# Attention and two MLP layers on one core: weight blocks without a cache in HBM, and a first down pass on half slabs

## The chip, the cores and the metric

One core of one Trainium2 chip runs the whole program. The metric is device microseconds of one execution, taken as the median of several runs; lower is better.

## The reference, cut to what matters

```python
# q, k, v: (4, 12, 448, 64); g_q, g_k: (64,); 1792 tokens of 768
q_n, k_n = rmsnorm(q, g_q), rmsnorm(k, g_k)
x = softmax(q_n @ k_n.T / 8) @ v          # per batch and head, then (1792, 768)
h = np.maximum(x @ w_in, 0.0)             # w_in  (768, 2048)
x = (h * h) @ w_out                       # w_out (2048, 768)
g = x @ w_gate                            # w_gate, w_val (768, 1536)
out = (g / (1 + np.exp(-g)) * (x @ w_val)) @ w_out2   # w_out2 (1536, 768)
```

The weights come in as 64-bit floats, so the kernel reads them as pairs of 32-bit words and builds 32-bit floats from them with integer operations. Each matrix product runs on TensorE in a reduced 32-bit format: an operand is split into a high part (rounded to that format) and a low part (the rest), and three products (high by high, high by low, low by high) are added up.

## The kernel before, in words

The kernel is one stream of instructions for each engine, in an order that is written out by hand in Python. Nothing is reordered later: an engine runs its own list in order and waits for other engines by semaphores. "Emitted" below means put at the end of such a list.

**Attention** (L363 to L796) runs over 24 pairs of heads, one iteration for each (the loop at L710). Per iteration TensorE makes a pass for the maxima (L543), the scores (L572), row sums (L608), transposes (L511, L552) and the product with v (L587, 16 matmuls). DVE (VectorE) reduces the maxima (L546, four per iteration) and makes the low parts of the transposed operands (L526, L530). POOL (GpSimd) normalises (L493) and adds up the exponentials (L578).

**The two up layers** (`up`, L940) use Strassen's scheme in Winograd's form: the weights of one quad (two slabs of 128 output columns, each 768 deep) are combined to seven blocks P1 to P7 of 128 x 384, and the tokens of a pair of batches (tp 0 or 1) to seven types B11, B21, B22, T1 to T4. A group is one block by one type: 9 matmuls of 128x128 by 448 columns (L871). The first layer has 8 quads, the second 12, so they have 112 and 168 groups. The types T1 to T4 need differences on DVE (`combine`, L120), a high part on ACT (ScalarE; L123) and a low part on DVE or POOL (L127), 1344 columns each. After a group DVE or ACT evicts PSUM (L834, L837). In before, the first two quads run for tp 0 alone at the start of a layer, and for tp 1 alone at its end. Their 14 blocks are made once, stored to HBM (`keep`, L281) and loaded twice through a ring of five buffers (`ring_loads`, L252 to L260).

**The two down layers** (`down`, L992) take the hidden blocks (128 x 448) back from HBM (`stage`, L967, L974), split each in `cleave` (L976: high part on ACT at L980, low part on POOL by the helper at L834) and multiply it with a split slab of weights: 18 matmuls (L1014) for one block, for four batches t after each other, over 16 or 12 slabs f. The slab of block (t=0, f) is converted just ahead of its use.

**Weights.** `stream` (L328) is a generator of all weight work: `convert` (L187) makes 32-bit floats of a slab of 128x768 by one ACT copy (L204) and three DVE operations (L206, L210, L214); sums of half slabs are made on DVE (L286); `block` (L270) splits a block by an ACT cast (L275) and a DVE subtraction (L276); `down_slab` (L315) splits a whole slab (L323 on ACT, L324 on DVE). `pump(budget)` (L343) emits the next operations of that generator up to a budget in planned microseconds; it is called after each group and each down step. In attention `prep_early(1)` (L351) does so for one DVE operation, at two places of each iteration from the third on:

```python
for c in range(NCH):
    if i > 0:
        maxpass(i + 1, c)
    scores(i, c)
    ...
    if c == 1:
        ...
        if i >= 3:
            prep_early(1)          # L732, in the middle of the scores
...
if i >= 3:
    prep_early(1)                  # L756, ahead of the row sums
```

Raw slabs are loaded by `load_raws` (L170, DMA issued at L180) into one buffer and a second that borrows space from the token array. All DMAs of the program but four tiny ones are issued in order by SP (SyncE); a wait ahead of one holds up those behind it.

Of the kernel before, what the change touches and what calls it, by code (L numbers as in the profile page):

```python
# [8 lines left out]
F32 = mybir.dt.float32  # L9
# [10 lines left out]
def kernel(  # L20
# [17 lines left out]
    P = 128  # L38
# [10 lines left out]
    RING = 5  # L49
    UNIT = 2 * KT * S  # L50
# [11 lines left out]

    def slot(s):
        return xacc[:, s * S:(s + 1) * S]
# [5 lines left out]
    units, flat = {}, {}  # L70

    def open_units(name, ids, side="left", apart=False):
        pool = ctx.enter_context(tc.tile_pool(name=name, bufs=1, side=side))
        for part in ([i] for i in ids) if apart else (ids,):
            t = pool.tile([P, len(part) * UNIT], F32R, tag=f"u{part[0]}", name=f"u{part[0]}")
            for n, i in enumerate(part):
                units[i] = t[:, n * UNIT:(n + 1) * UNIT]
            flat[part[0]] = t

    where = (  # L80
# [4 lines left out]
    )  # L85
    HUNIT = (10, 7)
    WHOME = ([(3, n) for n in range(7)] + [(0, n) for n in range(5)] + [(7, n) for n in range(4)],
             [(3, n) for n in range(7)] + [(11, 0), (12, 0), (13, 0), (0, 0), (0, 1)])
# [5 lines left out]
    free = []  # L94
    state = {"turn": 1, "used": 0, "raw": 0, "debt": 0.0, "late": False}
# [4 lines left out]

    def part_hi(t, kk):
        name = {(0, 0): "B11", (0, 1): "B21", (1, 1): "B22"}[t % 2, kk // KT]
        k = kind(0, t // 2, name)
        nc.scalar.copy(k[:, 0, kk % KT * S:(kk % KT + 1) * S], slot(t * KD + kk))

    def part_lo(t, kk, eng=None):
        name = {(0, 0): "B11", (0, 1): "B21", (1, 1): "B22"}[t % 2, kk // KT]
        k = kind(0, t // 2, name)
        cut = slice(kk % KT * S, (kk % KT + 1) * S)
        (eng or nc.vector).tensor_tensor(  # L110
            out=k[:, 1, cut], in0=slot(t * KD + kk), in1=k[:, 0, cut].bitcast(F32), op=ALU.subtract
        )

    def combine(tp, name, eng=None):
# [5 lines left out]
        (eng or nc.vector).tensor_tensor(out=slots3(*o), in0=slots3(*a), in1=slots3(*b), op=ALU.subtract)  # L120

    def hi3(name, tp, ph=0):
        nc.scalar.copy(kind(ph, tp, name)[:, 0], home3(tp, name))  # L123

    def lo3(name, tp, ph=0, eng=None):
# [4 lines left out]
        if name[0] == "T":  # L130
            t, h = home[name]
            s = (2 * tp + t) * KD + h * KT
            free.extend(x for x in range(s, s + KT) if not 12 <= x < 16 and x < 20)
            state["late"] |= (t, h, tp) == (1, 1, 1)

    def both(name, tp, ph=0, eng=None):
        hi3(name, tp, ph)
        lo3(name, tp, ph, eng)
# [13 lines left out]
    def row_slab(w, f):  # L152
        w, e = words(w)
        return w[f * P:(f + 1) * P, :].rearrange("p (a f) -> p a f", a=KD)
# [5 lines left out]
    raws, convs, ssum, ring = [], [], [], []  # L160
    slabs = []
    for ph in range(2):
        for n, (w, g) in enumerate(ups[ph]):
            for f in range(2):
                slabs.append((col_slab(w, 2 * g + f), 0 if n < 4 or f else 1))
        for f in range(NF[ph]):
            slabs.append((row_slab(downs[ph], f), 1 - f % 2))
# [921 lines left out]
```

## Time and profile before

| what | value |
|---|---|
| median of 3 runs | 1334.46 us (1333.95 to 1338.06) |
| the profiled execution's own time | 1340.05 us |
| its span in the profile | 1338.3 us |
| busy share of the span, PE / DVE / ACT / POOL | 91% / 55% / 42% / 37% |
| mean granted TensorE clock | 0.963 of full speed |
| moved by DMA | 166.81 MB |

Matmuls are pipelined, so the busy share of PE overstates its work; how many matmuls ran in a stretch says more. The shares of the other engines are averages over stages that have different limits: attention ends at about 290 us, the first up layer at 537, the first down layer at 817, the second up layer at 1156.

### The profile page before, as it was taken

To read this page: it belongs to the slowest core of one execution; us is meant where nothing else is said; L and a number is where in the kernel's file an instruction comes from. 1 tells how busy PE (TensorE), PEld (TensorE's weight loads), DVE (VectorE), ACT (ScalarE), POOL (GpSimd) and SP (SyncE) were. 2 spreads that over 40 slices of the span, in tenths; PEclk is the share of its full clock that TensorE was granted. 3 is DMA by queue.
4 is the path that set the end of the run, shared out by engine and by line. 5 is a ranking of instruction groups with operands and counts; after the bars stand their busy time and mean duration, and the time that the engine had idled before them with its cause. 6 is when DMAs were issued, how large, how long until landed. Compare 5 with 4: busy or idle time off the path is not lost.

```text
span 1338.3 us, 17283 instructions
## 1 busy us (share of the span) xinstructions
PE 1220.1 (91%) x6416; PEld 1018.4 (76%) x6416; DVE 731.9 (55%) x900; ACT 559.2 (42%) x917; POOL 500.8 (37%) x423
## 2 busy tenths in 40 slices
PE   8989888897799997976799999799999998799998
PEld 5555544466699996865599999699999997689998
DVE  7777878857767637766101104776776655740000
ACT  6767766563455544423122224333343332331221
POOL 6887877644010001221235456311302312333332
PEclk9999989898999998987799999899999999999999
DMA  5334444224334448746522213322233227643331
GB/s 161 109 114 130 125 119 134 87 90 142 126 103 142 158 128 281 227 155 216 184 77 62 62 42 95 108 97 80 89 102 110 89 73 240 226 139 102 110 106 46
DMA packets 109189, 166.81 MB, mean 125 GB/s; under 512 B 13105, under 2 KB 94769, under 8 KB 109105
## 3 DMA queue, kind: packets, MB, share of 16 engines
q1 hardware_dynamic: 108784, 165.71, 39.4%
q8 instruction: 50, 0.82, 0.3%
q14 instruction: 35, 0.28, 0.1%
q10 hardware_dynamic: 320, 0.00, 0.0%
HBM read 123.21 MB, written 42.29 MB: 124 GB/s over the span
## 4 chain that ended last, share of the span: by engine, by line
PE 42%; DVE 4%; DMA 3%; issue 2%; ACT 1%; POOL 0%; SPq 0%; POOLq 0%; ACTq 0%; DVEq 0%
PE ps L1014 22%; PE ps L871 20%; DMA keep<-ring 1%; DVE conv L210 1%; DMA xacc<-hid 1%; DVE xacc L120 1%; DVE conv L214 1%; DVE conv L206 1%; DMA xacc<-in_moe_w_out_dram 1%; ACT u L123 0%; DMA ring<-keep 0%; DMA raw<-in_moe_w_val_dram 0%; POOL u L834 0%; DVE xacc L834 0%; ACT conv L204 0%
## 5 line engine op out<-in xcount | busy, mean ns | idle before, releaser
L871 PE MATMUL ps<-u,ring 128*128 128x448 f32 x2520 | 538.8, 375 | 46.5 <-DVE xacc L834 27.4
L871 PEld LDWEIGHTS ps<-u,ring 128*128 128x128 f32 x2520 | 483.8, 193 | 101.7 <-DVE xacc L834 25.2
L1014 PE MATMUL ps<-u,u 128*128 128x448 f32 x2016 | 427.3, 373 | 32.2 <-ACT u L980 14.5
L1014 PEld LDWEIGHTS ps<-u,u 128*128 128x128 f32 x2016 | 386.4, 192 | 72.8 <-ACT u L980 18.7
L834 POOL TENSOR_TENSOR u<-xacc,u 128x448 fp32r<-128x448 f32 x112 | 134.3, 1202 | 322.3 <-ACT u L980 322.3
L834 POOL TENSOR_TENSOR xacc<-xacc 128x448 f32<-128x448 f32 x76 | 99.9, 1318 | 391.4 <-ACT xacc L837 274.5
L980 ACT CAST u<-xacc 128x448 fp32r<-128x448 f32 x112 | 63.2, 565 | 250.2 <-PE ps L1014 200.2
L1026 DVE COPY xacc<-ps 128x448 f32<-128x448 f32 x24 | 14.8, 623 | 270.6 <-PE ps L1014 270.6
L834 DVE TENSOR_TENSOR xacc<-ps,xacc 128x448 f32<-128x448 f32 x188 | 115.7, 619 | 79.4 <-PE ps L871 63.8
L578 POOL TENSOR_TENSOR sg<-p 112x896 f32<-112x896 f32 x46 | 97.9, 2130 | 40.4 <-ACT p L574 40.4
L546 DVE TENSOR_REDUCE mxz<-s 112x2 f32<-112x896 f32 x96 | 100.0, 1082 | 20.8 <-PE s L543 20.7
L276 DVE TENSOR_TENSOR ring<-conv,ring 128x384 fp32r<-128x384 f32 x100 | 69.8, 700 | 66.7 <-ACT ring L275 66.5
L837 ACT ACTIVATE xacc<-xacc 128x448 f32<-128x448 f32 x132 | 76.1, 576 | 66.5 <-DVE xacc L834 64.8
L837 ACT ACTIVATE xacc<-ps 128x448 f32<-128x448 f32 x108 | 58.0, 543 | 94.2 <-PE ps L871 70.2
L574 ACT ACTIVATE p<-s 112x896 f32<-112x896 f32 x96 | 87.5, 920 | 19.2 <-PE s L572 15.3
L275 ACT CAST ring<-conv 128x384 fp32r<-128x384 f32 x100 | 50.7, 509 | 77.7 <-PE ps L871 45.5
L587 PE MATMUL s<-p,v 112*64 112x448 f32 x384 | 80.0, 559 | 0.0
L572 PE MATMUL s<-th 64*112 64x448 f32 x576 | 76.5, 369 | 1.4 <-DVE th L530 0.8
L206 DVE TENSOR_SCALAR conv<-conv 128x768 int32<-128x768 int32 x68 | 51.8, 761 | 35.1 <-ACT conv L204 33.5
L127 POOL TENSOR_TENSOR u<-xacc,u 128x1344 fp32r<-128x1344 f32 x15 | 48.7, 3249 | 31.5 <-ACT u L123 27.5
L493 POOL TENSOR_TENSOR qk<-raw,r 112x512 f32<-112x512 f32 x46 | 59.9, 1306 | 1.0
L210 DVE SCALAR_TENSOR_TENSOR conv<-raw,conv 128x768 int32<-128x768 int32 x42 | 59.1, 1406 | 1.2
(75 smaller groups left out, 973.8 us busy)
## 6 DMA issues: line engine op xcount, KB each, us to landing
hid<-xacc SPq DMA_DIRECT2D x112, 224.0 KB
xacc<-hid SPq DMA_DIRECT2D x112, 224.0 KB
ring<-keep SPq DMA_DIRECT2D x56, 384.0 KB
keep<-ring SPq DMA_DIRECT2D x28, 384.0 KB
xacc<-in_moe_w_out_dram SPq DMA_DIRECT2D x14, 768.0 KB
raw<-in_moe_w_out_dram SPq DMA_DIRECT2D x14, 768.0 KB
raw<-in_moe_w_in_dram SPq DMA_DIRECT2D x12, 768.0 KB
raw<-in_moe_w_gate_dram SPq DMA_DIRECT2D x8, 768.0 KB
```

The costliest lines, as they stand in the source:

```text
L206: nc.vector.tensor_scalar(out=ci, in0=ci, scalar1=3, scalar2=0x7FFFFFFF, op0=ALU.logical_shift_left, op1=ALU.bitwise_and)
L210: nc.vector.scalar_tensor_tensor(out=ci, in0=high, scalar=-0x80000000, in1=ci, op0=ALU.bitwise_and, op1=ALU.bitwise_or)
L276: nc.vector.tensor_tensor(out=r[:, 1], in0=src, in1=r[:, 0].bitcast(F32), op=ALU.subtract)
L546: nc.vector.tensor_reduce(out=mxz[:, c, 0:P:D], in_=ps[:CP, :, :S], op=ALU.max, axis=AX.X)
L572: nc.tensor.matmul(ps[:CP, a, :S], lhs, rhs, start=(w == 0), stop=(w == 3))
L574: nc.scalar.activation(out=p, in_=ps[:CP, :, :S], func=AF.Exp)
L578: nc.gpsimd.tensor_tensor(out=sg, in0=p_t[pi, 2 * w], in1=p_t[pi, 2 * w + 1], op=ALU.add)
L587: nc.tensor.matmul(ps[s, :S], v_t[pi][:, a, c * D:(c + 1) * D], p[:, a, :], start=(c == 0), stop=(c == NCH - 1),)
L834: eng.tensor_tensor(out=o, in0=a, in1=b, op=op)
L837: nc.scalar.activation(out=slot(s), in_=src, func=func)
L871: nc.tensor.matmul(ps, w[:, wi, kk * P:(kk + 1) * P], xk[:, xi, kk * S:(kk + 1) * S], start=bool(first and mm == 0), stop=(mm == 3 * KT - ...
L1014: nc.tensor.matmul(ps[o], w[:, wi, o * P:(o + 1) * P], h[:, hi], start=(f == 0 and n == 0), stop=(f == nf - 1 and n == 2),)
```

## The change

The cache in HBM is gone. At the start of an up layer P1 and P2 of the first two quads run for tp 0 and then for tp 1, and all other blocks run for both pairs at once, straight from the ring. The types of tp 1 are therefore made in the first 18 groups, by a list of due groups. There are five conversion buffers instead of three. The raw buffer of attention is a tile of its own; later raws lie in the token array (slots 16 to 23).

In the down layers the weights come as half slabs (128 x 384). The first pass takes batches 0 and 1 together: for half 0 and then half 1 of the outputs, and for each f, both hidden blocks meet one half slab (2 x 3 outputs x 3 = 18 matmuls). Their hidden blocks are loaded and split twice, once for each half. Batches 2 and 3 follow with whole rows as before. The low part of a hidden block is made on DVE, no longer on POOL. In attention the first of the two `prep_early(1)` calls is left out, and T1 and T2 of tp 0 are split after it.

```diff
     for ph in range(2):
         for n, (w, g) in enumerate(ups[ph]):
...
-        for f in range(NF[ph]):
-            slabs.append((row_slab(downs[ph], f), 1 - f % 2))
+        for h in range(2):
+            for f in range(NF[ph]):
+                loads.append((row_half(downs[ph], f, h), ((h * NF[ph] + f) % 4,)))
...
+    def load_raws(lag=2):
+        while nsent["n"] < len(loads):
+            i = nsent["n"]
+            src, at_ = loads[i]
+            if i >= state["limit"] or i - len(turned) > 3 or not all(valid(b) for b in at_):
                 return
+            for n in range(max(0, i - 8), i):
+                if set(loads[n][1]) & set(at_) and turned.get(n, 1 << 30) + lag > clock["n"]:
+                    return
...
+            sent[i] = clock["n"]
...
+    def convert(i, c, cost):
...
+        arrived = lambda: i in sent and clock["n"] >= sent[i] + 3
...
+        yield act(lambda: nc.scalar.activation(out=c, in_=high.bitcast(F32), func=AF.Copy, scale=TINY), gate=arrived)
+        yield dve(0.6 * cost, lambda: nc.vector.tensor_scalar(
+            out=ci, in0=ci, scalar1=3, scalar2=0x7FFFFFFF, op0=ALU.logical_shift_left, op1=ALU.bitwise_and))
+        yield dve(cost, stt, ci, high, -0x80000000, ALU.bitwise_and)
+        yield dve(cost, stt, ci, low, 29, ALU.logical_shift_right)
+        turned[i] = clock["n"]
...
     def block(entry, src):
-        n = at[entry][0]
...
-        if how == "store":
-            c = cache[ph, p, q_] = mem["keep"].tile([P, 2 * KH], F32, tag=f"c{ph}{p}{q_}", name="keep")
-            nc.sync.dma_start(out=c, in_=r.bitcast(F32).rearrange("p h n -> p (h n)"))
-            used(n)
+        yield act(nc.scalar.copy, r[:, 0], src, gate=lambda: state["used"] >= n - RING + 1)
+        yield dve(0.55, minus, r[:, 1], src, r[:, 0].bitcast(F32))
...
+            for n in range(2 * NF[ph]):
+                c = convs[i % NCONV][:, :KH]
...
+                ops = convert(i, c, 0.5)
+                i += 1
+                op = next(ops)
+                yield op[:4] + (lambda g=op[4], n=n, ph=ph: g() and state["down"] >= 100 * ph + n // 6,)
+                for k, op in enumerate(ops):
+                    yield op
+                    if k == 1 and late:
+                        yield late
+                        late = None
...
+                yield act(nc.scalar.copy, t[:, 0], c)
+                late = dve(0.55, low_half, ph, n, t, c)
...
     def pump(budget):
         state["debt"] = min(state["debt"] + budget, budget + 1.5)
-        while state["debt"] > 0:
-            cost = next(steps, None)
...
+        while True:
+            op = peek()
+            if op is None or (op[4] and not op[4]()) or (op[0] == "dve" and state["debt"] <= 0):
                 return
-            state["debt"] -= cost
+            state["debt"] -= run_op()
...
             for i in range(np_):
+                clock["n"] += 5
+                load_raws()
...
-                        if i >= 3:
-                            prep_early(1)
...
-                elif i == np_ - 2:
-                    both("T1", 0)
-                elif i == np_ - 1:
-                    both("T2", 0)
...
         def up(ph):
...
-            for n, (p, q_) in enumerate(paired):
-                step(ph, [(p, q_, 0)], n0[0] + n)
...
+            todo = [("P1", 0, 0), ("P1", 1, 0), ("P2", 0, 0), ("P2", 1, 0),
+                    ("P1", 0, 1), ("P1", 1, 1), ("P2", 0, 1), ("P2", 1, 1)]
+            todo += [(p, q_, tp) for p, q_ in paired[4:] + mid for tp in range(2)]
+            last = len(ups[ph]) - 1
+            for p, q_, tp in todo:
+                step(ph, p, q_, tp, 1.0 if state["down"] < 100 * ph else 1.6)
...
         def cleave(ph, t, f):
...
             nc.scalar.copy(k[:, 0], src)
-            tt(nc.gpsimd, k[:, 1], src, k[:, 0].bitcast(F32), ALU.subtract)
+            tt(nc.vector, k[:, 1], src, k[:, 0].bitcast(F32), ALU.subtract)
...
         def down_open(ph):
...
+            dn_seq[:] = [[(t, f) for t in range(2)] for _ in range(2) for f in range(nf)]
+            dn_seq.extend([(t, f)] for t in (2, 3) for f in range(nf))
...
-                pump(3.2)
+                pump(2.1)
...
+        plan_types(0, [
+            (1, "h", 0, "T1", None), (1, "l", 0, "T1", None), (1, "h", 1, "B11", None), (1, "l", 1, "B11", None),
+            (2, "h", 1, "B21", None), (3, "h", 0, "T3", None), (3, "l", 0, "T3", g), (3, "l", 1, "B21", None),
+            (4, "c", 1, "T1", None), (5, "h", 1, "T1", None),
...
```

In the list at the end, "c" is a combination, "h" a high part on ACT, "l" a low part (on POOL where `g` stands, else on DVE), and the first number is the group after which it is emitted.

## Rows read from the trace of the kernel before

**Rows 1.** Stretches: engine busy and (records), PEclk, DMA share, GB/s
```profile
290.10:536.70 246.60, 221.59 (x1012) 197.81 (x1009) 159.80 (x215) 127.01 (x220) 40.18 (x27) 0.94 0.49 154
536.70:817.20 280.50, 250.50 (x1153) 224.03 (x1151) 86.15 (x93) 75.81 (x123) 96.96 (x69) 0.94 0.38 121
600.00:663.00 63.00, 40.85 (x150) 33.52 (x149) 27.29 (x36) 16.26 (x31) 10.35 (x9) 0.80 0.63 214
663.00:817.00 154.00, 153.65 (x753) 142.32 (x754) 12.74 (x12) 35.12 (x55) 70.97 (x49) 0.99 0.21 57
817.20:1157.00 339.80, 318.29 (x1521) 287.50 (x1520) 229.70 (x309) 124.30 (x210) 94.27 (x65) 0.98 0.37 120
850.00:1117.00 267.00, 267.00 (x1286) 242.44 (x1285) 175.06 (x255) 92.89 (x169) 65.02 (x52) 0.99 0.31 99
```

**Rows 2.** Timeline of PE in attention: the product with v of some iterations
```profile
32.47 3.23 PE L587 MATMUL s<-p,v 112*64 112x448 f32 x16
42.16 3.23 PE L587 MATMUL s<-p,v 112*64 112x448 f32 x16
...
99.35 3.23 PE L587 MATMUL s<-p,v 112*64 112x448 f32 x16
113.31 3.23 PE L587 MATMUL s<-p,v 112*64 112x448 f32 x16
122.95 3.23 PE L587 MATMUL s<-p,v 112*64 112x448 f32 x16
...
268.79 3.23 PE L587 MATMUL s<-p,v 112*64 112x448 f32 x16
```

**Rows 3.** Timeline of DVE in attention: weight steps
```profile
106.25 2.16 DVE L276 TENSOR_TENSOR ring<-ssum,ring 128x384 fp32r<-128x384 f32 x1 [1.14 <-ACT ring L275]
...
118.97 0.55 DVE L286 TENSOR_TENSOR conv<-conv,ssum 128x384 f32<-128x384 f32 x1
...
145.20 3.62 DVE L206 TENSOR_SCALAR conv<-conv 128x768 int32<-128x768 int32 x1
```

**Rows 4.** Timeline of PE: waits at the edges of the up layers
```profile
363.25 37.06 PE L871 MATMUL ps<-u,ring 128*128 128x448 f32 x166 [5.21 <-DVE xacc L834]
...
849.50 20.68 PE L871 MATMUL ps<-u,ring 128*128 128x448 f32 x90 [7.36 <-DVE xacc L834]
```

**Rows 5.** The chain that ended last, in the first down layer
```profile
636.20 4.04 DMA keep<-ring
```

**Rows 6.** Timeline of ACT and DVE in the first down layer: one weight slab
```profile
555.87 0.83 ACT L323 CAST u<-conv 128x768 fp32r<-128x768 f32 x1 [3.07 <-DVE conv L214]
...
556.61 0.91 ACT L204 ACTIVATE conv<-xacc 128x768 f32<-128x768 f32 x1
...
557.62 0.55 DVE L206 TENSOR_SCALAR conv<-conv 128x768 int32<-128x768 int32 x1
...
558.21 1.82 DVE L210 SCALAR_TENSOR_TENSOR conv<-xacc,conv 128x768 int32<-128x768 int32 x1
...
560.06 0.96 DVE L214 SCALAR_TENSOR_TENSOR conv<-xacc,conv 128x768 int32<-128x768 int32 x1
561.05 0.83 ACT L323 CAST u<-conv 128x768 fp32r<-128x768 f32 x1 [3.07 <-DVE conv L214]
```

**Rows 7.** Groups of instructions: busy us, mean ns, then idle before
```profile
L834 DVE TENSOR_TENSOR xacc<-ps,xacc 128x448 f32<-128x448 f32 x188 | 115.7, 619 | 79.4 <-PE ps L871 63.8 <-ACT xacc L837 8.1 <-POOL xacc L834 7.5
...
L980 ACT CAST u<-xacc 128x448 fp32r<-128x448 f32 x112 | 63.2, 565 | 250.2 <-PE ps L1014 200.2 <-DMA xacc<-hid 36.0 <-issue 13.3
...
L275 ACT CAST ring<-conv 128x384 fp32r<-128x384 f32 x100 | 50.7, 509 | 77.7 <-PE ps L871 45.5 <-DVE conv L214 19.9 <-DVE conv L286 6.9
L127 POOL TENSOR_TENSOR u<-xacc,u 128x1344 fp32r<-128x1344 f32 x15 | 48.7, 3249 | 31.5 <-ACT u L123 27.5 <-issue 3.5
...
L120 DVE TENSOR_TENSOR xacc<-xacc 128x1344 f32<-128x1344 f32 x16 | 37.4, 2339 | 33.2 <-POOL u L127 33.2
...
L286 DVE TENSOR_TENSOR conv<-conv,conv 128x384 f32<-128x384 f32 x20 | 11.0, 551 | 0.0
```

More of the change, by code (lines that the diff above doesn't have):

```diff
@@ L49 @@
     RING = 5
+    NCONV = 5
     UNIT = 2 * KT * S
@@ L93 @@
     home = {"B11": (0, 0), "B21": (0, 1), "B22": (1, 1), "T1": (0, 0), "T2": (1, 1), "T3": (1, 0), "T4": (0, 1)}
-    free = []
-    state = {"turn": 1, "used": 0, "raw": 0, "debt": 0.0, "late": False}
+    loose = set()
     def home3(tp, name):
@@ L130, in lo3 @@
         if name[0] == "T":
[L131 to L138, printed above, removed]
+            release(tp, name)
     def split(n):
@@ L168 @@
-    turned = {"slab": 0}
-    def load_raws():
-        while state["raw"] < len(slabs):
-            i = state["raw"]
-            src, r = slabs[i]
-            if (r == 1 and not state["late"]) or i > turned["slab"] + 1:
-                return
-            if any(slabs[n][1] == r for n in range(turned["slab"], i)):
-                return
-            dst = raws[r]
-            if src.dtype == I32:
-                nc.sync.dma_start(out=dst.rearrange("p (a f) -> p a f", a=KD), in_=src)
-            else:
-                nc.sync.dma_start(
-                    out=dst.bitcast(F32)[:, :KD * P].rearrange("p (a f) -> p a f", a=KD), in_=src
-                )
-            state["raw"] += 1
@@ L813, in moe @@
         due = []
-        clock = {"n": 0}
+        types = []
         def later(n, fn, *args):
@@ L911, in after @@
                 later(1, finish_sum, ph, q_, tp, ij, s)
-        def step(ph, group_args, n, extra=()):
-            for p, q_, tp in group_args:
-                group(ph, p, q_, tp, n)
-                if (p, q_, tp) == group_args[-1]:
-                    used(n)
-                clock["n"] += 1
-                run_due()
-                after(ph, p, q_, tp)
-                while drain and drain[0][0] <= clock["n"]:
-                    drain.pop(0)[1]()
-                if types:
-                    types.pop(0)()
-                pump(1.6 if ready["down"] >= 2 * ph else 1.0)
@@ L940, in up, with step @@
[L940 to L959 removed]
+        def step(ph, p, q_, tp, rate):
+            group(ph, p, q_, tp)
+            if tp == 1:
+                assert at[ph, p, q_] == state["used"]
+                state["used"] += 1
+            clock["n"] += 1
+            run_due()
+            load_raws()
+            while types and types[0][0] <= clock["n"]:
+                types.pop(0)[1]()
+            after(ph, p, q_, tp)
+            while drain and drain[0][0] <= clock["n"]:
+                drain.pop(0)[1]()
+            pump(rate)
@@ new lines, in up, with stage @@
+            for args in dn_seq[1]:
+                cleave(ph, *args)
+        dn, hl, dn_seq, dn_list = {}, {}, [], []
+        count = {}
+        held = {}
+        def stage(ph, upto):
+            nf = NF[ph]
+            while count["s"] < len(dn_list) and dn_list[count["s"]][0] <= upto:
+                i, t, f = dn_list[count["s"]]
+                if i < 2 * nf:
+                    s = next((s for s in free if 3 <= s < 6 or 9 <= s < 16), None)
+                    if s is None:
+                        return
+                    free.remove(s)
+                    held[t, f] = s
+                else:
+                    if i == 2 * nf:
+                        assert not any(set(a) & {2, 3} for n, (_, a) in enumerate(loads) if n in sent and n not in turned)
+                        loose.difference_update(range(20, 24))
+                    s = 20 + i % 4
+                dn[t, f] = slot(s)
+                nc.sync.dma_start(out=slot(s), in_=hid[ph][f, t])
+                count["s"] += 1
```

561 lines of the change are left out of this document (290 added, 271 removed), and 4 rows, old and new, of the table where.

## The prediction

> **What bounds the kernel now.** I began with the stretches, because the shares over the whole span mix stages with different limits. The reader should look for stretches in which the count of matmuls is as high as it gets: 1286 in 267.00 us in the middle of the second up layer, 0.2076 us each, and 753 in 154.00 us late in the first down layer, 0.2045 us each [rows 1]. There TensorE has no gap. At these rates the work of the MLP stages is 1008 x 0.2076 = 209.3 (first up), 1152 x 0.2045 = 235.6 (first down), 1512 x 0.2076 = 313.9 (second up) and 864 x 0.2045 = 176.7 us (second down). The first three stages last 246.6, 280.5 and 339.8 us [rows 1], so they lose 37.3, 44.9 and 25.9: 108.1 us in all. The second down layer loses nothing but its end. Neither DVE nor DMA is busy throughout: the loss lies at the edges of the stages.
>
> The timeline of PE then shows the edges: up layers wait 5 to 7 us at a time for DVE while the types are made [rows 4]. The chain of waits shows stores to the cache one after the other, this one of 4.04 us and four like it [rows 5], in a stretch of 63 us that ran 150 matmuls and had a granted clock of 0.80 [rows 1].
>
> Last I read attention by iterations. One without any weight step lasts 42.16 - 32.47 = 9.69 us, one with short steps 122.95 - 113.31 = 9.64, another 113.31 - 99.35 = 13.96 [rows 2]. What differs is the weight step in the middle of the scores: 0.55 us in the one, 2.16 us for the same 384 columns in the other [rows 3]; it stands ahead of two of the four maxima that TensorE needs next. The 19 iterations from 42.16 to 268.79 take 226.6 us [rows 2] where 19 x 9.7 is 184.3: 42 us lost.
>
> **The change, part by part.**
>
> *Attention: -34 us.* The step in the middle goes. Nine of the 19 iterations look like the one at 99.35, with a middle step of 1.25 to 4.79 us; together they are 35.5 us over 9.7. I take nearly that, 34. The other step stays: 12 conversion and 6 split operations, one per iteration, which fit (each of four slabs takes four iterations, load included). It is not free: one such step took 3.62 us [rows 3], four of 18 were over 3 us, and the low parts of the operands wait behind it; that iteration was 2.5 us too long. Bounds: 42 if everything goes, 15 if other operations are hit as often half the time. Moving T1 and T2 out costs nothing here and is counted below.
>
> *Start of the first up layer: 9 us lost in place of some 25.* No ring loads, and P1 and P2 need only types made early. New is a rush on ACT and DVE: within 18 groups three combinations at 2.34 us, five low parts on DVE, and six on POOL at 3.25 us [rows 7]. Three places can stop TensorE. The eviction of P2 of quad 1 takes a slot that POOL's first low part has just read; behind it on ACT stand T1's high part and the copies that the second P1 pair needs: some 2 us. T2 of tp 1 is emitted at group 10 behind T3 on DVE and needed at group 13: some 3. The raw slabs of quad 2 need slots that POOL's last low part reads; 6 x 3.25 and four additions put that at about 41 us, landing and conversion at 52 to 57, where group 28 starts at 28 x 1.87 = 52: some 4. That load waits on SP, and the stores of hidden blocks queue behind it; their slots are reused only some ten evictions later. Bounds: 2 and 20.
>
> *End of the first up layer and first pass of the first down layer: 16 us.* The stores and reloads go, and with them their waits. What comes is the half slab. In before a whole slab is a loop between ACT and DVE: cast, copy, three DVE operations, next cast, 561.05 - 555.87 = 5.18 us [rows 6], while 18 matmuls take 18 x 0.2045 = 3.68. The half has no row. From below its operations are half of the whole's, from above the same. DVE operations on 384 columns took 0.551 and the ACT cast 0.509 [rows 7], so I take 0.58 with the gap for three DVE operations, 0.53 for cast and copy, and 0.37 for the shift (whole: 0.55 [rows 6]). A half then is 0.37 + 3 x 0.58 = 2.11 us on DVE, and after its last operation DVE waits for cast and next copy, 1.06. The new pump gives 2.1 of planned 1.85 per half, that is 8 halves in 7 steps. Each step also has two hidden blocks: two ACT casts of 0.565 and, now on DVE, two subtractions of about 0.62 [rows 7]. Per step DVE is busy 8/7 x 2.11 + 2 x 0.64 = 3.69 and idle some 0.7, since the subtractions fill part of the 1.06. So a step lasts 4.4 us, 0.7 more than TensorE's.
>
> The halves begin ten groups before the end. With four raw buffers, each back after five to six groups, 7 are done by then; they and ten evictions take 7 x 2.7 + 6.2 = 25 us on DVE where TensorE has 10 x 1.87 = 18.7: 6.5 late. 25 halves are left, 22 steps, 22 x 0.7 = 15.4. The blocks are split two steps ahead, a lead of 2 x 3.68 - 1.85 = 5.5. Together 15.4 + 6.5 - 5.5 = 16. The change of half at step 16 needs six banks evicted with two free: 2 us more. Traffic is no bound: a step loads 2 x 224 + 8/7 x 384 = 887 KB in 4.4 us, 202 GB/s, where 214 were moved before [rows 1].
>
> [...]
>
> *Later passes of the first down layer: nothing.* One subtraction of 0.62 per step of 3.68 on DVE beside the next layer's weights; should its cover go, nine low parts on POOL could each hold it up to 3.25 us [rows 7].
>
> *First to second up layer: 4 us lost in place of some 12* [rows 4]. The same rush without the raws: T1 comes first, T2 is again close at group 13. Bounds 1 and 10.
>
> *End of the second up layer and its down layer: 12 us, and 2 for the change of half.* As above with 24 halves: 17 left, 15 steps, 10.5 + 6.5 - 5.5. Before it was some 16.
>
> Sum: losses after 9 + 16 + 2 + 4 + 12 + 2 = 45, against 108.1: -63. With attention -97. From the span of 1338.3 that is 1241.3; outside the span lay 1340.05 - 1338.3 = 1.75, so 1243 for such an execution. The median of the runs shown is 5.6 us below the profiled time, so I predict 1237.
>
> **The rivals.**
>
> (a) *The loop is hidden.* If the order on ACT and DVE leaves no idle time, a step takes 3.69 and the passes lose some 4 us each: 1237 - 20 = 1217. For it: DVE's busy time alone just fits. Against it: the whole-slab loop left DVE idle at each cast. Chance 0.14.
>
> (b) *Attention stays slow,* because the remaining step or the reductions themselves run into POOL as often: 1237 + 34 = 1271. For it: the step of 3.62 us [rows 3]. Against it: it stands beside the product with v, 3.23 us of TensorE [rows 2]. Chance 0.12.
>
> (c) *Subtractions held by POOL.* With the lead used up, nine low parts at 3.25 us [rows 7] cost 29 us: 1266. Against it: the lead recovers once the halves are done. Chance 0.06. [...]
>
> (d) *Slower than before.* The half costs what the whole did: 5.18 us of loop [rows 6], since fixed costs or late raws, not columns, set it. A step is then 8/7 x 5.18 + 1.85 = 7.8 us, and 37 steps lose 3.4 more each: 1237 + 125 = 1362. It decides from a step of 4.4 + 97 / 37 = 7.0 us on. Against it: 384 columns at 0.55 [rows 7]. Chance 0.05.
>
> (e) *The schedule isn't kept:* the four slabs aren't done when attention ends, since each waits for its load. Then the first groups wait for some 18 operations, 20 us: 1257. Chance 0.03.
>
> **How the numbers follow.** The forecast has 0.60 and 1237, with its own range 1212 to 1262 from the bounds of attention and the starts. The range over the cases: below, attention 42 and losses of 20, 1204; above, attention 15 and losses of about 80, 1290. Only (d) and the tails lie outside. A measurement of this kernel can tell about 0.3%, 4 us. All cases but (d) are faster: 0.92 with a little off for mixtures; 0.02 within, 0.06 slower.
>
> **What would show it.** Right: iterations of attention near 9.7 us all through, attention ending near 256 us; steps of about 4.4 us in both first passes with PE waiting for DVE's subtraction, ACT casts waiting for the third DVE operation; no wait of over 4 us at the starts of up layers; up-layer rate still 0.2076. Wrong: iterations of 12 us and more in attention; PE waiting for raw DMA or, late in a down layer, for subtractions that last over 2 us; steps of 3.7 us (then (a)) or over 5.

## The result and the profile after

| | before | changed |
|---|---|---|
| median | 1336.26 us (1333.95 to 1341.86, 4 runs) | 1260.87 us (1259.04 to 1263.33, 4 runs) |
| span of the profiled execution | 1338.3 us | 1259.1 us |
| its own time | 1340.05 us | 1261.24 us |
| busy PE / DVE / ACT / POOL | 91 / 55 / 42 / 37% | 95 / 64 / 47 / 30% |
| moved by DMA | 166.81 MB | 146.64 MB |

The ratio is 0.9431, interval 0.9396 to 0.9467. A first look at where the 79.2 us of span went is by the stretches of [rows 1], here from the kernel after: first up layer, first down layer, 19.5 steps of its first pass, second up layer, second down layer.

```profile
253.21:489.69 236.48, 212.96 (x1013) 193.58 (x1009) 164.02 (x240) 128.37 (x232) 51.68 (x29) 0.95 0.40 127
489.69:743.24 253.55, 243.31 (x1153) 217.12 (x1153) 131.26 (x229) 96.23 (x179) 28.50 (x9) 0.99 0.42 130
512.87:596.80 83.93, 76.98 (x352) 64.65 (x351) 60.77 (x122) 39.64 (x84) 0.00 (x0) 1.00 0.62 196
743.24:1061.55 318.31, 309.59 (x1514) 285.51 (x1512) 229.71 (x330) 122.75 (x220) 87.28 (x61) 0.98 0.31 99
1061.55:1259.10 197.55, 185.07 (x864) 163.92 (x864) 81.94 (x151) 58.28 (x115) 2.39 (x2) 0.98 0.43 137
```

Against [rows 1] attention is 36.9 us shorter (290.10 to 253.21), the first up layer 10.1, the first down layer 27.0, the second up layer 21.5; the second down layer is 16.3 longer, since its first pass now pays for the second layer's edge. Taking off the work at the prediction's rates (209.3, 235.6, 313.9 and 176.7 us), the four stages lose 27.2, 17.9, 4.4 and 20.9: 70.4, of which 4.6 were there before at the very end. So 65.8 stand against the 45 forecast. This is a net figure: where nothing held TensorE, its matmuls ran faster after the change than at the prediction's rates (last section), which hides about 11 us, an estimate from the starts of the groups; the edges themselves cost some 77.

The product with v in attention, the instruction of [rows 2]:

```profile
42.00 3.23 PE L609 MATMUL s<-p,v 112*64 112x448 f32 x16
51.70 3.23 PE L609 MATMUL s<-p,v 112*64 112x448 f32 x16
...
217.57 3.23 PE L609 MATMUL s<-p,v 112*64 112x448 f32 x16
229.86 3.23 PE L609 MATMUL s<-p,v 112*64 112x448 f32 x16
```

Nineteen iterations from 42.00 take 187.9 us where they took 226.6. Most are 9.7 long; the one ahead of 229.86 is the longest with 12.29. What stands in it on DVE is not the weight step but a combination (L124) beside POOL:

```profile
215.94 6.75 DVE L124 TENSOR_TENSOR xacc<-xacc 128x1344 f32<-128x1344 f32 x1
```

The waits of PE at the edges, where [rows 4] had 5.21 and 7.36 (the number in brackets is the idle time before the instruction, then what ended it):

```profile
259.04 3.93 PE L881 MATMUL ps<-xab,ring 128*128 128x448 f32 x18 [1.92 <-ACT xacc L849]
269.62 5.48 PE L881 MATMUL ps<-xbb,ring 128*128 128x448 f32 x18 [3.00 <-ACT xacc L849]
289.00 0.74 PE L881 MATMUL ps<-xbt,ring 128*128 128x448 f32 x1 [4.60 <-ACT xbt L141]
293.47 3.36 PE L881 MATMUL ps<-xbt,ring 128*128 128x448 f32 x8 [3.73 <-DVE xbt L145]
481.32 3.70 PE L881 MATMUL ps<-xat,ring 128*128 128x448 f32 x9 [8.06 <-DVE xacc L846]
489.69 0.47 PE L1058 MATMUL ps<-xat,xab 128*128 128x448 f32 x1 [2.00 <-ACT xat L1010]
497.13 3.27 PE L1058 MATMUL ps<-xat,xab 128*128 128x448 f32 x7 [3.01 <-ACT xat L1010]
565.80 0.88 PE L1058 MATMUL ps<-xat,xbb 128*128 128x448 f32 x3 [2.06 <-ACT xacc L1080]
...
1054.11 6.38 PE L881 MATMUL ps<-xat,ring 128*128 128x448 f32 x18 [7.32 <-ACT xat L367]
```

Four waits stand at the start of the first up layer. The longest, 8.06 and 7.32, stand ahead of the last groups of each up layer: an eviction (L846) and a half slab's cast (L367) that came late.

Some waits cost more than their own length. TensorE's granted clock stood at two levels from 253.21 us on, 1.00 in 3819 and 0.50 in 191 of 4024 windows of 0.25 us, and between them only in the 14 in which it changed; behind the wait of 8.06 us it stood at the lower one (the column after POOL's is the granted clock):

```profile
481.32:485.22 3.90, 3.70 (x10) 2.78 (x10) 2.39 (x5) 1.91 (x5) 0.00 (x0) 0.50 0.95 358
```

The nine matmuls that start at 481.32 last 3.70 us where nine take 1.82 to 1.86 at the full clock. The stretches from 293.47 to 296.60 (behind the waits of 4.60 and 3.73), from 497.13 to 501.00 (behind 3.01) and from 1054.10 to 1057.50 (behind 7.32) show 0.50 as well; in between, TensorE ran on and the rows are back at 1.00. An estimate from windows of 1 us, TensorE's busy time times what was missing of the full clock, gives some 16 us for the four stages after the change and some 29 before it.

What holds the start is on POOL, DVE and ACT:

```profile
261.91 4.45 POOL L145 TENSOR_TENSOR xat<-xacc,xat 128x1344 fp32r<-128x1344 f32 x1 [0.65 <-ACT xat L141]
263.87 3.90 DVE L124 TENSOR_TENSOR xacc<-xacc 128x1344 f32<-128x1344 f32 x1
266.40 0.55 ACT L849 ACTIVATE xacc<-ps 128x448 f32<-128x448 f32 x1 [4.11 <-POOL xat L145]
...
280.94 4.16 POOL L145 TENSOR_TENSOR xbb<-xacc,xbb 128x1344 fp32r<-128x1344 f32 x1 [4.92 <-ACT xbb L141]
285.13 2.47 DVE L124 TENSOR_TENSOR xacc<-xacc 128x1344 f32<-128x1344 f32 x1 [2.97 <-POOL xbb L145]
289.82 1.19 DVE L227 TENSOR_TENSOR ring<-conv,ring 128x384 fp32r<-128x384 f32 x1 [2.22 <-ACT ring L367]
290.93 2.48 DVE L145 TENSOR_TENSOR xbt<-xacc,xbt 128x1344 fp32r<-128x1344 f32 x1
```

The low part of T3 on POOL and the combination of T1 on DVE run beside each other and both last longer (3.25 and 2.34 on average in [rows 7]; a combination alone took 1.55 us in this trace); the eviction on ACT waits 4.11 us for POOL's slot, as forecast. The last four lines are the chain behind the waits of 4.60 and 3.73: the combination of T2 waits 2.97 us for POOL's low part of B22, and T2's own low part stands behind a weight operation (L227) that waits 2.22 us for ACT.

The loop of one half slab, which answers to the 5.18 us of [rows 6]:

```profile
528.53 0.51 ACT L367 CAST xbb<-conv 128x384 fp32r<-128x384 f32 x1 [2.11 <-DVE conv L224]
528.95 0.54 ACT L243 ACTIVATE conv<-xacc 128x384 f32<-128x384 f32 x1
529.39 1.02 ACT L1010 CAST xat<-xacc 128x448 fp32r<-128x448 f32 x2
529.52 0.36 DVE L244 TENSOR_SCALAR conv<-conv 128x384 int32<-128x384 int32 x1 [1.02 <-ACT conv L243]
529.91 0.56 DVE L224 SCALAR_TENSOR_TENSOR conv<-xacc,conv 128x384 int32<-128x384 int32 x1
530.39 0.55 DVE L227 TENSOR_TENSOR xbb<-conv,xbb 128x384 fp32r<-128x384 f32 x1
530.86 1.15 DVE L846 TENSOR_TENSOR xat<-xacc,xat 128x448 fp32r<-128x448 f32 x2
...
531.93 0.55 DVE L224 SCALAR_TENSOR_TENSOR conv<-xacc,conv 128x384 int32<-128x384 int32 x1
532.51 0.52 ACT L367 CAST xbb<-conv 128x384 fp32r<-128x384 f32 x1 [2.11 <-DVE conv L224]
...
535.44 0.51 ACT L367 CAST xab<-conv 128x384 fp32r<-128x384 f32 x1 [1.96 <-DVE conv L224]
```

A half with a step's two blocks (L1010, L846) takes 532.51 - 528.53 = 3.98 us, one without blocks 535.44 - 532.51 = 2.93. DVE idles 1.02 behind the copy, ACT 2.11 behind the last integer operation. The first pass ran 351 matmuls, 19.5 steps, in 83.93 us: 4.30 per step, forecast 4.4. This row takes in the wait of 2.06 at the change of half and, at its end, about three steps behind the last halves at some 3.7; the steps beside halves come to 4.3 without that wait too.

### The profile page after: what moved, and what is told of

The parts are those of the page before. It is cut to its first block, busy times and chain, and to the rows that moved or that the text cites. A ratio compares the mean times of both kernels' runs of the same rounds, so it can differ in the third digit from the quotient of the medians.

```text
span 1259.1 us, 17643 instructions
## 1 busy us (share of the span) xinstructions
PE 1194.9 (95%) x6416; PEld 1003.0 (80%) x6416; DVE 810.5 (64%) x1177; ACT 592.0 (47%) x1029; POOL 376.1 (30%) x314
## 2 busy tenths in 40 slices
DMA packets 109190, 146.64 MB, mean 116 GB/s; under 512 B 13104, under 2 KB 101936, under 8 KB 109104
## 4 chain that ended last, share of the span: by engine, by line
PE 42%; DVE 4%; ACT 2%; issue 1%; DMA 1%; POOL 0%; SPq 0%; ACTq 0%; DVEq 0%
PE ps L881 23%; PE ps L1058 20%; DVE conv L224 2%; DMA xacc<-hid 1%; DVE conv L244 1%; ACT conv L243 0%; POOL xab L145 0%; DVE xab L846 0%; DVE xacc L846 0%; ACT xab L1010 0%; DVE xbt L846 0%; ACT xacc L849 0%; DVE xbt L227 0%; SPq L998 0%; DVE xacc L124 0%
## 5 line engine op out<-in xcount | busy, mean ns | idle before, releaser
L846 POOL TENSOR_TENSOR xacc<-xacc 128x448 f32<-128x448 f32 x76 | 101.1, 1338 | 357.2 <-ACT xacc L849 260.4
L881 PE MATMUL ps<-xat,ring 128*128 128x448 f32 x720 | 160.5, 374 | 15.4 <-DVE xacc L846 8.1
L881 PEld LDWEIGHTS ps<-xat,ring 128*128 128x128 f32 x720 | 139.0, 194 | 27.9 <-issue 8.4
L224 DVE SCALAR_TENSOR_TENSOR conv<-xacc,conv 128x384 int32<-128x384 int32 (+1 forms) x184 | 149.5, 813 | 4.4
L846 DVE TENSOR_TENSOR xacc<-ps,xacc 128x448 f32<-128x448 f32 x188 | 115.4, 619 | 54.4 <-PE ps L881 52.7
L881 PE MATMUL ps<-xbt,ring 128*128 128x448 f32 x540 | 119.8, 370 | 8.7 <-ACT xbt L141 4.6
L227 DVE TENSOR_TENSOR ring<-conv,ring 128x384 fp32r<-128x384 f32 x120 | 83.7, 699 | 65.4 <-ACT ring L367 63.8
L881 PE MATMUL ps<-xbb,ring 128*128 128x448 f32 x540 | 118.5, 369 | 3.0 <-ACT xacc L849 3.0
L881 PE MATMUL ps<-xab,ring 128*128 128x448 f32 x540 | 117.0, 366 | 1.9 <-ACT xacc L849 1.9
L881 PEld LDWEIGHTS ps<-xbt,ring 128*128 128x128 f32 x540 | 102.4, 190 | 18.2 <-ACT xbt L141 5.0
L881 PEld LDWEIGHTS ps<-xbb,ring 128*128 128x128 f32 x540 | 102.6, 190 | 11.7 <-ACT xacc L849 3.4
L881 PEld LDWEIGHTS ps<-xab,ring 128*128 128x128 f32 x540 | 101.3, 188 | 11.1 <-ACT xacc L849 2.3
L367 ACT CAST ring<-conv 128x384 fp32r<-128x384 f32 x120 | 60.9, 510 | 100.9 <-PE ps L881 59.3
L568 DVE TENSOR_REDUCE mxz<-s 112x2 f32<-112x896 f32 x96 | 99.7, 1086 | 11.9 <-PE s L565 11.6
L846 DVE TENSOR_TENSOR xat<-xacc,xat 128x448 fp32r<-128x448 f32 x65 | 44.7, 701 | 93.2 <-ACT xat L1010 93.2
L600 POOL TENSOR_TENSOR sg<-p 112x896 f32<-112x896 f32 x46 | 98.9, 2151 | 16.3 <-ACT p L596 16.3
L1010 ACT CAST xat<-xacc 128x448 fp32r<-128x448 f32 x65 | 35.6, 563 | 95.7 <-PE ps L1058 70.4
L846 DVE TENSOR_TENSOR xab<-xacc,xab 128x448 fp32r<-128x448 f32 x48 | 29.3, 623 | 78.6 <-ACT xab L1010 74.3
L244 DVE TENSOR_SCALAR conv<-conv 128x384 int32<-128x384 int32 (+1 forms) x96 | 51.6, 537 | 43.5 <-ACT conv L243 41.5
```

The source lines that it names most:

```text
L224: nc.vector.scalar_tensor_tensor(out=out, in0=in0, scalar=scalar, in1=out, op0=op, op1=ALU.bitwise_or)
L227: nc.vector.tensor_tensor(out=out, in0=a, in1=b, op=ALU.subtract)
L244: yield dve(0.6 * cost, lambda: nc.vector.tensor_scalar(out=ci, in0=ci, scalar1=3, scalar2=0x7FFFFFFF, op0=ALU.logical_shift_left, op1=ALU ...
L367: fn(*args)
L568: nc.vector.tensor_reduce(out=mxz[:, c, 0:P:D], in_=ps[:CP, :, :S], op=ALU.max, axis=AX.X)
L600: nc.gpsimd.tensor_tensor(out=sg, in0=p_t[pi, 2 * w], in1=p_t[pi, 2 * w + 1], op=ALU.add)
```

## The experiments

All are edits of the changed kernel; times are medians, to be held against 1260.6 us of the first run. The kernel before, run again beside each batch, took 1338.8 to 1341.9 us, so medians of different batches can be compared within some 3 us. Line numbers in runs that delay the half slab's subtraction differently are 3 lower.

**The changed kernel once more.** 

> The changed kernel itself, as the measure for the runs beside it: 1256 to 1266 us. Attention ends near 253 us, the first down pass takes half slabs at some 4.0 us each.

Measured: 1260.6 us (1256.51 to 1265.81), 0.9403 (0.9377 to 0.9428). Its waits are the same ones: 1.66, 2.87, 4.78 and 3.73 at the start, 8.12 and 7.33 at the two ends.

**The one weight step of attention, moved into the middle of the scores.**

```diff
                     if c == 1:
...
+                        if i >= 3:
+                            prep_early(1)
...
-                if i >= 3:
-                    prep_early(1)
```

> The one weight step per iteration of attention is moved from behind the scores into their middle; number and kind of steps stay. Theory (the place decides: a step that stands ahead of two of the four maxima holds TensorE whenever POOL makes it long): many iterations of 11 to 14 us in place of 9.7, attention ends at 265 to 285 us and the whole is 12 to 32 us longer. Rival (the number of steps decides, one in place of two): attention ends at 253 to 256 us and the whole is the same within 4 us.

Measured: 1282.58 us, 0.9563 (0.9531 to 0.9594): 22 us more. Here is one such iteration on DVE, POOL and PE:

```profile
48.39 2.10 POOL L600 TENSOR_TENSOR sg<-p 112x896 f32<-112x896 f32 x1 [1.49 <-ACT p L596]
49.14 1.76 DVE L244 TENSOR_SCALAR conv<-conv 128x768 int32<-128x768 int32 x1 [1.52 <-ACT conv L243]
50.82 2.08 DVE L568 TENSOR_REDUCE mxz<-s 112x2 f32<-112x896 f32 x2
52.05 0.96 PE L630 MATMUL s<-sg,onef 112*32 112x448 f32 x8 [2.62 <-DVE mxz L568]
```

The weight step waited for ACT's copy, then ran beside POOL, and the maxima (L568) came behind it; this iteration took 12.4 us. Attention ended at 272.23 us, against 253.63 in the run above. With as many steps in all, at the other place, half of the 36.9 us of attention's gain is gone: the place costs this much whatever the count. Where the other half of the gain comes from this run does not separate.

**The half slab's subtraction ahead of the next half's first DVE operation.**

```diff
-                for k, op in enumerate(ops):
-                    yield op
-                    if k == 1 and late:
-                        yield late
-                        late = None
                 if late:
                     yield late
+                for op in ops:
+                    yield op
```

> The subtraction that ends a half slab is emitted ahead of the next half's first DVE operation, beside ACT's cast and copy, in place of between its second and third. Theory (the ends of the up layers and the first down passes are bound by the loop of ACT and DVE, in which DVE is idle for about 1.04 us per half): a half takes 3.5 us in place of 4.0, some 32 + 24 halves, less what the other subtractions filled already: 8 to 24 us shorter. Rival (the loop is not what binds; raws or hidden blocks arrive late): the same within 3 us.

Measured: 1252.94 us, 0.9348 (0.9324 to 0.9372), 8 us less. In some halves the subtraction now fills the time in which DVE waited for the copy:

```profile
521.84 0.52 ACT L364 CAST xbb<-conv 128x384 fp32r<-128x384 f32 x1 [1.83 <-DVE conv L224]
522.25 0.55 ACT L243 ACTIVATE conv<-xacc 128x384 f32<-128x384 f32 x1
522.38 0.56 DVE L227 TENSOR_TENSOR xbb<-conv,xbb 128x384 fp32r<-128x384 f32 x1 [0.58 <-ACT xbb L364]
...
525.38 0.51 ACT L364 CAST xbb<-conv 128x384 fp32r<-128x384 f32 x1 [1.65 <-DVE conv L224]
```

This half took 3.54. In the first down pass only three did and two took 3.72; twelve took 4.10 to 4.14, longer than the 4.00 of the control, and those without blocks 2.59 in place of 2.92. The 32 casts span 121.0 us in place of 125.2. So the order in the loop through ACT does set the half, as the theory had it, but the 3.5 us that it forecast for every half came for few of them, and the whole gain is at the theory's lower end.

**Three edits of the start of the first up layer.** First the low part of B22 on DVE:

```diff
-            (9, "h", 1, "B22", None), (9, "l", 1, "B22", g), (10, "c", 1, "T3", None),
+            (9, "h", 1, "B22", None), (9, "l", 1, "B22", None), (10, "c", 1, "T3", None),
```

> The low part of type B22 of tp 1 in the first layer goes from POOL to DVE. Theory (T2's combination overwrites the space that POOL reads for that low part, so DVE, ACT and TensorE wait for POOL): TensorE's two waits ahead of the second P6 group, 4.60 and 3.73 us, fall under 2 us each, and the whole is 3 to 7 us shorter. Rival (DVE has too much to do there): one more operation of 1.55 us on DVE leaves the waits as long or makes them longer, 0 to 2 us more.

Measured: 1261.65 us, 0.9412 (0.938 to 0.9444), waits 4.98 and 3.73 as before. The theory fell: without POOL's low part, the two combinations lasted 4.08 us together beside an eviction's addition on POOL (2.01 us). Then everything of groups 9 to 11 in the order of need on DVE:

```diff
-            (9, "h", 1, "B22", None), (9, "l", 1, "B22", g), (10, "c", 1, "T3", None),
-            (10, "c", 1, "T2", None), (10, "h", 1, "T2", None), (11, "l", 1, "T2", None),
+            (9, "c", 1, "T3", None), (9, "h", 1, "B22", None), (9, "l", 1, "B22", None), (9, "c", 1, "T2", None),
+            (9, "h", 1, "T2", None), (9, "l", 1, "T2", None),
```

> At the start of the first layer the combinations T3 and T2 of tp 1, B22's low part (on DVE) and T2's high and low part are all emitted after group 9, one behind the other, where they stood at groups 9 to 11 between weight operations. Theory (after the run with B22's low part on DVE alone changed nothing): it is the order on DVE that makes T2 late, weight operations and their waits for ACT stand between its combination and its low part. Then T2's low part ends some 5 us earlier, TensorE's waits of 4.8 and 3.7 us fall to 4 together, the whole is 4 to 7 us shorter. Rival (DVE simply has too much to do, in any order): the two waits together stay over 7 us and the whole is the same within 3 us.

Measured: 1258.99 us, 0.9393 (0.9356 to 0.943). The two waits fell from 8.51 to 4.62, so the order on DVE did make T2 late, but a new one of 2.92 for a ring cast came behind them. Last, the low part of T3 of the first pair on DVE:

```diff
-            (3, "l", 0, "T3", g),
+            (3, "l", 0, "T3", None),
```

> T3's low part of tp 0 goes from POOL to DVE. Theory (ACT's Relu of P2 of quad 1 writes a slot that POOL's low part still reads, and the copies of the second P1 pair stand behind it on ACT): TensorE's wait of 2.9 us ahead of the second P2 pair falls under 1, the whole is 2 to 5 us shorter. Rival (DVE is the one that is late): the wait stays or grows, the whole is the same within 2 us.

Measured: 1258.57 us, 0.9395 (0.9361 to 0.943). The first two waits fell from 4.53 to 3.03, and the one that was to fall under 1 us is 2.20; in the whole none of the three edits can be told from nothing. At this start moving one operation mostly moves the wait.

**Planned time at the end of the up layers back to 1.0 per group.**

```diff
-                step(ph, p, q_, tp, 1.0 if state["down"] < 100 * ph else 1.6)
+                step(ph, p, q_, tp, 1.0)
```

> The pump gives 1.0 and not 1.6 after each of the last groups of an up layer. Theory (ACT and DVE have a fixed amount to do from there to the end of the first down pass, and TensorE waits for it whichever side it falls on; no lead exists that could absorb it): the waits of 8.1 us ahead of the last groups shrink to under 3, some three half slabs fewer are ready, and the whole is the same within 4 us. Rival (crowding the last groups is itself the loss): 6 to 15 us shorter.

Measured: 1244.78 us, 0.9302 (0.9255 to 0.935), 16 us less by the medians, 13 by the ratios. My theory fell and the rival holds: the wait of 8.12 is 3.92 now, and so is that of 7.33.

```profile
480.02 2.63 PE L881 MATMUL ps<-xat,ring 128*128 128x448 f32 x9 [3.92 <-DVE xacc L846]
1043.44 5.47 PE L881 MATMUL ps<-xat,ring 128*128 128x448 f32 x18 [3.91 <-DVE xacc L846]
```

Six halves instead of eight were ready at the start of the down layer and the last was cast 3 us later, yet the end of the pass came earlier. Work made ahead of need stood ahead of evictions that TensorE needed.

**The low part of a hidden block on POOL again.**

```diff
-            tt(nc.vector, k[:, 1], src, k[:, 0].bitcast(F32), ALU.subtract)
+            tt(nc.gpsimd, k[:, 1], src, k[:, 0].bitcast(F32), ALU.subtract)
```

> The low part of a hidden block is made on POOL, as before the change. Theory (POOL and DVE take turns, so what DVE is spared comes back as longer operations): half slabs still take 3.7 to 4.2 us each, DVE's operations on xacc and conv become longer than 0.56 us, the whole is between 4 us shorter and 8 us longer. Rival (POOL is a free helper and DVE was too full): a half falls to 3.3 us or less, 10 to 20 us shorter.

Measured: 1295.68 us, 0.968 (0.9633 to 0.9727), 35 us more, far outside what I had allowed.

```profile
509.83 0.51 ACT L367 CAST xbt<-conv 128x384 fp32r<-128x384 f32 x1 [2.92 <-DVE conv L224]
...
512.00 1.28 POOL L846 TENSOR_TENSOR xbt<-xacc,xbt 128x448 fp32r<-128x448 f32 x1
...
512.29 1.39 DVE L224 SCALAR_TENSOR_TENSOR conv<-xacc,conv 128x384 int32<-128x384 int32 x1
...
514.08 0.55 DVE L224 SCALAR_TENSOR_TENSOR conv<-xacc,conv 128x384 int32<-128x384 int32 x1
514.66 0.51 ACT L367 CAST xab<-conv 128x384 fp32r<-128x384 f32 x1 [2.92 <-DVE conv L224]
```

The theory's sign was right, its size wrong: the integer operation of 0.56 us lasts 1.39 beside POOL, and a half 4.83 where at most 4.2 was allowed. That operation started at 512.29, while POOL's low part ran from 512.00 to 513.28, and ended at 513.68, 0.40 us behind POOL's, as the theory's turns would have it; the one at 514.08, with no record of POOL beside it, lasted 0.55. TensorE also waited 32 times for POOL's low parts themselves, 25.4 us in all.

**One half per step in the first down passes.**

```diff
-                pump(2.1)
+                pump(1.85 if i < 2 * nf else 2.1)
```

> Edit: the changed kernel with the planned time given out per step of the two first down passes cut from 2.1 to 1.85, which is one half slab's planned time, so one half per step instead of 8 in 7. Theory (surplus): a half made ahead of need takes ACT and DVE ahead of the blocks that TensorE needs next, so the steps that make 8 in 7 last 4.3 us, while a step with one half lasts about the half's own 4.0 us. Then 25 halves take 25 x 4.0 and the 7 steps behind them 3.65 each, 125.6 us for the first pass in place of 22 x 4.3 + 10 x 3.65 = 131: 5 us less here, 4 less in the second layer, 1248 to 1255 us where the control has 1260.6; casts of the high part (L367) 4.0 us apart as before, one in each step. Rival: a step lasts 4.3 us because of its blocks and banks, whatever the halves; spreading 25 halves over 25 steps then costs 25 x 4.3 + 7 x 3.65 = 133, that is 0 to 5 us more, 1260 to 1266.

Measured: 1247.96 us, 0.9307 (0.9269 to 0.9345), 12.6 us less. Behind the first two of the pass the casts are 3.98 to 4.00 us apart, but for 5.05 at the change of half. In the control three halves of the first pass had no blocks beside them and lasted 2.92 each; 3 x 2.92 = 8.8 us by which, as I read it, they held up the blocks. The theory holds, with more gained than it forecast. The first down layer went from 256.2 to 248.1 us and the rest behind the second up layer from 198.4 to 188.5.

**The two best single edits together, and five together.** 

> Edit: the two single edits that helped, together: planned time of 1.0 in the last groups of the up layers (alone -16 us) and the half's subtraction ahead of the next half's first operation on DVE (alone -8 us). Theory (they act at different places: the one keeps halves out of the way of the evictions at the end of the up layers, the other shortens each half by 0.13 us): the two add, -24 us, 1233 to 1241 us, halves some 3.85 us apart in the first down pass. Rival (both only give DVE and ACT room at the same few microseconds before the down layer): together no more than the larger, 1242 to 1248 us.

Measured: 1236.6 us (1235.12 to 1242.8), 0.9225 (0.919 to 0.9259). The gains add, as far as the intervals tell: 16 + 8 = 24. This beats both kernels and is the best version measured.

> Edit: both single edits that helped (planned time 1.0 at the end of the up layers, the half's subtraction earlier), one half per step in the first down passes (1.85), T3 of the first token pair low on DVE, and the operands of groups 9 to 11 of the first up layer in the order of need on DVE. Theory (surplus, and waits that add): 1237 for the first two, 5 to 9 less for one half per step, 2 to 4 less at the start of the first up layer: 1222 to 1233 us. Rival (one half per step brings nothing, and the two orders at the start only move a wait, as each did alone): 1234 to 1245 us.

Measured: 1248.04 us, 0.9297 (0.926 to 0.9333). Neither theory had that: three more edits, of which one alone gave 12.6, and 11 us lost. The casts are 4.57 us apart in every step of the first pass, the first down layer takes 256.5 us.

**The five without the delayed subtraction's new place.** 

> Edit: the five edits together without the earlier subtraction (planned time 1.0 at the end of the up layers, one half per step in the first down passes, T3 of the first token pair low on DVE, groups 9 to 11 of the first up layer in the order of need on DVE). Theory (the order inside a step made the five lose: with one half per step the delayed subtraction came behind the two blocks, so DVE stood 1.49 us in each step behind ACT's cast, copy and first block, and a step of 4.57 us came out): without it DVE has the half's own loop again, casts of the high part 4.0 us apart, stage of the first down layer 246 to 250 us in place of 256.5, in all 1226 to 1238 us. Rival (one half per step doesn't go with a small stock of halves: planned time 1.0 leaves fewer ready, and a step that can't run ahead waits at both ends): casts 4.3 us or more apart again, first down layer 253 us or more, 1242 to 1250 us.

Measured: 1245.81 us, 0.9301 (0.9267 to 0.9335): the rival's time. Casts are 4.45 us apart, the first down layer takes 253.9 us. One step on ACT and DVE:

```profile
525.70 0.51 ACT L367 CAST xbb<-conv 128x384 fp32r<-128x384 f32 x1 [2.56 <-DVE conv L224]
526.11 0.56 ACT L243 ACTIVATE conv<-xacc 128x384 f32<-128x384 f32 x1
526.57 1.02 ACT L1010 CAST xbt<-xacc 128x448 fp32r<-128x448 f32 x2
527.16 1.16 DVE L846 TENSOR_TENSOR xbt<-xacc,xbt 128x448 fp32r<-128x448 f32 x2 [1.50 <-ACT xbt L1010]
528.24 0.35 DVE L244 TENSOR_SCALAR conv<-conv 128x384 int32<-128x384 int32 x1
...
530.15 0.52 ACT L367 CAST xbb<-conv 128x384 fp32r<-128x384 f32 x1 [2.56 <-DVE conv L224]
```

These are the same operations as in the loop shown above, in another order. There DVE did the next half's shift and more while ACT cast the blocks, and idled 1.02; here the blocks' subtractions are next in DVE's list, and it idles 1.50 behind cast, copy and block cast. The difference, 4.45 - 3.98, is one block cast on ACT (526.57 + 0.45 is where the next starts, by the 1.02 for two). With one half per step the list is cut at the same place of the half in every step, so a good cut (with 1.85 alone) or a bad one (here) is kept for the whole pass. That the cut does it is read from the traces; what moved it, fewer halves in stock or the planned time left over at the start of the pass, was not tried alone, and neither were 1.0 and 1.85 without the other two edits. Some 6 us of this run are not the edit's: from 1010.11 to 1039.87 us nine of its matmuls took 1.860 us on average, where nine of the control's took 1.824 from 1011.50 to 1046.15, an estimate of 6 us for the 1512 of the second up layer.

## Why the prediction was right, and where it was not

The time, 1260.9, is inside the range, only 1 us below the upper end of the forecast's own range of 1212 to 1262; by the profiled executions it is 1261.2 against 1243, 18.2 too low. The time alone would not tell the forecast case: the rivals at 1257 and 1266 lie nearer than 1237. What tells it are the stages: attention ended near the forecast, the steps took 4.3 us, and the first down passes waited where they were said to. One sign of being right failed, since a wait at the start of the first up layer was 4.60 us and none over 4 was allowed.

*Attention, -34:* measured -36.9 us to its end, and half of it confirmed by moving the step back (attention 18.6 us longer, the whole 22). The one iteration that was 2.6 us too long was not held by the remaining step, as the prediction allowed, but by a combination of 6.75 us beside POOL.

*Start of the first up layer, 9:* it lost 18. Group 28 starts at 323.52, so 28 groups took 70.3 us where 52 are their work. The first two of the three places were right and too small: the eviction behind POOL's low part cost 1.92 + 3.00 where I had 2, T2 cost 4.60 + 3.73 where I had 3. The durations were not what failed: there are four combinations in these groups and not three, and their 3.90 + 1.55 + 2.47 + 1.54 us come to 9.46 where four of the mean in [rows 7] make 9.36. What failed is that each place was priced by itself: T2 waits for POOL's low part, then for ACT, then behind a weight operation, and these add up along the chain. And about 4.5 of the 18 are none of the three places, but the lower granted clock behind the waits, a term that the prediction put at nothing. The third place, raw slabs late, does not show.

*End of the first up layer and first pass, 16:* it lost some 30: about 13 up to the first step, 8.06 + 2.00 of it in two waits; 6.6 in the first 4.5 steps, 3.01 of it in a wait; and 83.93 - 19.5 x 3.68 = 12.2 in the 19.5 steps of the row, of which 2.06 belong to the change of half. In the first two of these the lower granted clock has an estimated 5.2. The step came out right (4.3, forecast 4.4; half 3.99, forecast 3.85; eight halves ready, forecast seven), but in part by luck: from 512.87 to 585.96 us, 16.6 steps beside halves, DVE was busy 53.11 us, 3.2 per step where 3.69 was forecast, and idle about 1.1 where 0.7 was, so two errors nearly cancel. The failed term is "+ 6.5 - 5.5": the lead of two steps that I subtracted never existed, because ACT and DVE come to the down layer late, so TensorE first waits for the backlog and then for the first blocks. That backlog comes in good part from halves emitted too eagerly, as the run with planned time 1.0 showed: 13 to 16 us, for both layers.

The start of one DVE operation on 384 columns lay 530.39 - 529.91 = 0.48 us ahead of the next one's, though the record lasts 0.56; the prediction had 0.58 with the gap. A half without blocks took 2.93 us where the prediction's terms, 2.11 + 1.06, make 3.17. The step did not get shorter by it, because DVE idled longer.

*Half change, 2:* 2.06. *Later passes, 0:* no wait at all in the trace from 597 to 743 us. *First to second up layer, 4:* one wait of 0.33 us; the three places of the first layer do not repeat, so I was too high.

*End of the second layer, 12 + 2:* with the line above 18 were forecast, and 4.4 + 20.9 - 4.6 = 20.7 were lost by the prediction's rate. But the second up layer gained some 7 by faster matmuls, so these edges cost about 27: 7.32 at the last groups, 3.39 at the half change, an estimated 6 by the lower granted clock, the rest in other waits and in steps. As in the first layer the forecast is some 13 too low, and the terms are the same: the lead that was subtracted, and matmuls behind a wait counted at the full rate.

*The median:* I took off 5.6 us because before's profiled execution had lain that far above its median; here the two differ by 0.4, so that shift was noise and no term.

*The rivals:* the hidden loop (1217) is out, since steps are 4.3. Attention staying slow (1271) is out. Subtractions held by POOL were forecast at 29 us for late passes, which did not occur; the run with POOL shows an integer operation on DVE held beside POOL (1.39 us in place of 0.56) and costs 35 where POOL is made to work in the pass, 25.4 of it waits of TensorE for POOL. The half costing the whole's 5.18 is out: 3.98. The schedule kept. No run put the cache or the whole slabs back by themselves, so how the gain at the edges divides among the parts of the change is read from the stretches and not shown by a run.

## What to carry to other kernels

A loop between two in-order engines is priced by its longest way round, not by busy time: one half slab and two blocks, the same operations, took 3.54, 3.98, 4.13 or 4.45 us, and the traces show a different order in each. Work prepared ahead of need has to wait its turn behind what the bound engine needs next, or else that stands behind it: two edits that gave it out more slowly were worth 13 to 16 us each, but they did not add. When a wait has several causes that share engines, moving one operation moves the wait, so price such a rush along its chain of waits and not by a sum of durations. And count a wait of TensorE with the matmuls behind it: in this trace they ran at half the clock behind the waits of 8.06, 7.32, 4.60 and 3.73, and 3.01 us.

## What was not expected of the hardware

Two stretches of nothing but matmuls at a granted clock of 1.00 had different rates, 485 and 495 matmuls in 100 us. Here is 100 us in the middle of the second up layer, before and after the change:

```profile
900.00:1000.00 100.00, 100.00 (x485) 90.84 (x484) 68.72 (x98) 37.08 (x67) 24.66 (x20) 1.00 0.29 95
850.00:950.00 100.00, 100.00 (x495) 92.66 (x495) 71.47 (x103) 37.56 (x68) 24.69 (x19) 1.00 0.32 100
```

Nine matmuls take 1.824 us in some stretches after the change and 1.860 in others, with no pattern by stage that I could find; this stays unexplained. A part of the second up layer's good result (4.4 lost, though one wait alone was 7.32) is this: its matmuls ran faster than the 0.2076 by which its work was counted.
